# Five h matmuls instead of nine ahead of batch 1's first pair of score tiles

## The chip, the cores and the metric

The kernel runs on one core of a Trainium2 chip. The metric is the device time of one execution in microseconds. The engines have these names in the profile: PE is TensorE (matmuls), PEld its weight loads, ACT is ScalarE, DVE is VectorE, POOL is GpSimd and SP is SyncE. In this kernel POOL mainly issues loads, and SP issues transposing transfers and stores.

## What is computed

Sigmoid attention over 8 batches, 12 heads, 448 positions and 64 channels; its output, as 3584 rows of 768, goes through a two-matrix MLP with SiLU.

```
scores = q @ k.T / sqrt(64) - log(448)
attn   = 1 / (1 + exp(-scores))
x      = (attn @ v), heads side by side      # 3584 x 768
h      = x @ w_in                            # 768 -> 2048
out    = (h * sigmoid(h)) @ w_out            # 2048 -> 768
```

## The kernel before

A **group** g is four heads of one batch: three groups a batch (`NQ`), 24 in all. A group has seven **units** of scores (`NCH`), each a score tile: `scores` (L216) issues four matmuls of 64 rows into a double PSUM bank `psc` (L223) and then one sigmoid on ACT (L230), after which the bank is free. The units are numbered n = 7g + ch. Batch 0 has units 0 to 20 and batch 1 has 21 to 41.

When the seven units of a group are through, `values` (L238) multiplies them with v: 28 matmuls into two single banks `pav` (L254), which DVE copies, scaled, into xT (L265). Three such groups make one batch's xT.

The **h unit** (`h_unit`, L282) is one block of 128 of the 2048 columns of h for one batch: six matmuls (L286) into a single bank `ph`. For batch 0 ACT then takes the sigmoid (L300, into a buffer `tx`), and DVE multiplies it with the bank's content into gTr (L301); the bank is free after that. For batch 1 one SiLU on ACT (L305) does both. There are 16 h units a batch. The fifth and sixth matmul of a unit need the last group's xT of that batch.

PSUM has eight banks. In this phase two pairs are the double banks for score tiles, and four are single banks, shared by `ph`, `pav` and the transposes' outputs `ptrk` and `ptrq` (`pe_transpose`, L186: 14 matmuls, L194, and two copies on DVE, L201). A new tile in a single bank waits until the tile that had the bank before is read out. Which bank a tile takes follows from the order in which the tiles stand in the program.

The order is written out by hand. Units 0 to 23 come first, each followed by what the table `behind` (L699) says; behind units 21 and 23 the first four matmuls of h units 0 and 1 of batch 0 are issued (`begin`, the generators in `early`). Then h of batch 0 is woven between the remaining score tiles of batch 1:

- `first_h` (L551) is a generator that issues h matmuls, batch 0's units and then batch 1's, and yields 189 (ns) for each one.
- `stretch(stream, ns)` (L731) adds ns to `due` and takes matmuls from the generator until `done`, the sum of what they yielded, has reached `due`. What one stretch takes too much is taken off the next, since both sums run on.
- `burst(n)` (L741) issues the score tiles n and n + 1 and then, if a group is waiting for them, its values. Bursts are called here by their first unit: 24, 26, ... 40. Behind burst 26 and burst 30 stand the k and q transposes of group 5; in burst 28 the values of group 3, in burst 36 those of group 4.
- Ahead of burst 24 stands one stretch, and one more behind each of the nine bursts, so ten in all. Then come the values of group 5 (L761), the rest of batch 0's h, and all of batch 1's h.

```
754      stream = first_h()
755      stretch(stream, 1600)
756      for n in range(NT_B + 3, 2 * NT_B, 2):
757          burst(n)
758          if n in (26, 30):
759              transposes(5, "k" if n == 26 else "q")
760          stretch(stream, 1600)
761      values_if_any()
762      for _ in stream:
763          pass
```

While the generator runs, it also issues some DVE work for later phases: sums of parts of w_in (L324) behind batch 0's later h units, sums of w_out (L475) behind batch 1's. Loads of q, k, v and the weights are issued by POOL in the order of the program; each waits for an earlier load on the same semaphore and, where its buffer was in use, for the last reader.

Behind this phase stand three more rounds for the other six batches (output projection of finished batches woven with the attention of the next two), in the same order whatever the first phase does.

Of the kernel before, what the change touches and what calls it, by code (L numbers as in the profile page):

```python
# [17 lines left out]
def kernel(  # L18
# [532 lines left out]
    def first_h():  # L551
        for b in range(2):
            for fc in range(NFC):
                yield from early[fc] if b == 0 and fc < 2 else h_unit(b, fc)
                if b == 0 and fc >= 10 or b == 1 and fc < 6:
                    next(in_sums)
                if b == 0:
                    continue
                if fc >= 2:
                    next(sums)  # L560
                if fc in by_h1:
                    for name in ("k", "q"):
                        dma_transpose(by_h1[fc], name, nc.vector.tensor_copy)
                    if by_h1[fc] == 8:

                        nc.gpsimd.tensor_copy(gate, qkT["q", 8][:1, 0, :1])
                        for to in (9, 10, 11):
                            load("kq", to)

    def sets(m):  # L570
        for g in range(0, NCH - 1, 2):
            step = out_set(
                block(m, g), row_blocks(m, g), block(m, g + 1), row_blocks(m, g + 1)
            )
            for i, ns in enumerate(step):
                if m == 0 and g == 0 and i in (10, 14):
                    next(sums)
                if m == 0 and g == 0 and i in (20, 28, 36, 44):
                    next(in_sums)
                yield ns  # L580
        if m % 2 == 1:
            g = NCH - 1
            yield from out_set(
                kept, row_blocks(m - 1, g), block(m, g), row_blocks(m, g), m == B // 2 - 1
            )
# [145 lines left out]
    def stretch(stream, ns, spent=0):  # L731
        nonlocal done, due
        due += ns
        done += spent
        while done < due:
            step_ns = next(stream, None)
            if step_ns is None:
                return
            done += step_ns
# [12 lines left out]
        return with_values  # L752

    stream = first_h()
    stretch(stream, 1600)
    for n in range(NT_B + 3, 2 * NT_B, 2):
        burst(n)
        if n in (26, 30):
# [9 lines left out]
    for m in range(B // 2 - 1):  # L768
        banks_for_attention(3)
        nc.scalar.activation(warm, bias_s, AF.Sigmoid)  # L770
        stream = sets(m)
# [74 lines left out]
```

## Time and profile before

| | us |
|---|---|
| timed runs before, median of 3 | 369.14 |
| timed runs before, lowest and highest | 368.26, 369.56 |
| the profiled execution | 368.01 |
| its span, first to last instruction | 366.1 |
| granted TensorE clock over the span | 1.000 |
| from burst 24's first matmul to batch 1's sixth h matmul | 29.70 to 58.08 |

How to read the views: the page gives for each engine the time that it was busy and its share of the span. The chain of waits is followed back from the last instruction, at each step to what released it; each row has a start, a length and what ran. The timeline gives for each engine merged rows: start, length until the last one ends, line, operation, output and inputs, count, and in brackets the idle time just ahead with what ended it. TensorE's matmuls are pipelined: a matmul of 448 columns is shown 0.35 us long, while the next one starts 0.19 us after it. So the starts tell the pace, and an idle time in brackets is shorter than the time lost.

### The profile page before, as it was taken

What the parts mean: (1) busy time and instruction counts of PE and PEld (TensorE: products, weight loads), DVE (VectorE), ACT (ScalarE), POOL (GpSimd) and SP (SyncE); (2) the same over time, 40 slices, a digit from 0 to 9 for tenths busy, and PEclk for the clock granted to TensorE, in tenths of its full rate; (3) what the DMA queues carried; (4) which work ended last, traced back from release to release, by engine and by line L of the source; (5) the groups of instructions that cost most, each with busy time, mean ns of one, the idle gap of its engine ahead of it and who ended that gap; (6) DMA issues with size and microseconds to landing.
All of it is one profiled execution on the core that took longest, in us unless ns stands there. A gap on an engine that the chain in (4) does not pass through costs nothing.

```text
span 366.1 us, 7649 instructions
## 1 busy us (share of the span) xinstructions
PE 357.9 (98%) x3036; PEld 186.1 (51%) x3036; DVE 252.1 (69%) x459; ACT 249.9 (68%) x339; POOL 77.5 (21%) x116
## 2 busy tenths in 40 slices
PE   8899999999999999999999999999999999999995
PEld 5454445545544555555555545554555555555552
DVE  3665569777657587867675768795756677797763
ACT  6998885479998755687877856679998856640000
POOL 8556522040060172000023046000100000000000
PEclk9999999999999999999999999999999999999999
DMA  8999999989989599007879669902853120003333
GB/s 133 197 204 204 204 204 203 172 125 163 163 115 211 120 119 185 3 0 143 109 131 192 118 139 161 115 2 53 167 96 88 25 63 0 3 0 88 86 87 86
DMA packets 65859, 42.80 MB, mean 117 GB/s; under 512 B 36128, under 2 KB 62496, under 8 KB 65824
## 3 DMA queue, kind: packets, MB, share of 16 engines
q0 software_dynamic: 27072, 22.58, 42.4%
q1 hardware_dynamic: 38320, 19.34, 27.1%
q8 instruction: 24, 0.39, 0.4%
q10 hardware_dynamic: 432, 0.39, 0.3%
q14 instruction: 11, 0.09, 0.1%
HBM read 45.61 MB, written 11.01 MB: 155 GB/s over the span
## 4 chain that ended last, share of the span: by engine, by line
PE 83%; DMA 12%; POOL 3%; issue 1%; DVE 1%; POOLq 0%; DVEq 0%
PE po L502 37%; PE psc L223 9%; PE pa L376 8%; PE pd L376 8%; PE pc L376 7%; PE pav L254 7%; PE ph L286 5%; DMA w_out_sb<-in_moe_w_out_dram 5%; PE pb L376 4%; DMA w_in_sb<-in_moe_w_in_dram 3%; DMA vf<-in_v_dram 2%; DMA qf<-in_q_dram 2%; POOL kf L124 1%; POOL w_out_sb L162 1%; POOL vf L124 1%
## 5 line engine op out<-in xcount | busy, mean ns | idle before, releaser
L230 ACT ACTIVATE attnT<-psc,bias_s 128x896 f16<-128x896 f32 x168 | 158.1, 1008 | 22.2 <-PE psc L223 21.8
L502 PEld LDWEIGHTS <-S 128*128 128x128 f16 x448 | 41.6, 98 | 35.4 <-issue 7.3
L223 PE MATMUL psc<-qT,kT 64*64 64x448 f16 x672 | 50.5, 362 | 0.9 <-ACT attnT L230 0.6
L265 DVE TENSOR_SCALAR xT<-pav 128x448 f16<-128x448 f32 x48 | 27.7, 619 | 29.8 <-PE pav L254 29.8
L124 POOL DMA_DIRECT2D vf<-in_v_dram x24 | 17.3, 723 | 130.8 <-PE pav L254 118.5
L502 PEld LDWEIGHTS <-gTr 128*128 128x128 f16 x336 | 31.2, 98 | 26.6 <-issue 7.9
L502 PE MATMUL po<-T,S 128*128 128x384 f16 x224 | 41.7, 327 | 0.0
L376 PEld LDWEIGHTS <-w_in_sb 128*128 128x128 f16 x288 | 27.9, 98 | 26.7 <-issue 1.1
L502 PE MATMUL po<-w_out_sb,gTr 128*128 128x384 f16 x224 | 41.5, 327 | 0.0
L502 PE MATMUL po<-w_out_sb,S 128*128 128x384 f16 x224 | 40.6, 326 | 0.0
L286 PE MATMUL ph<-xT,w_in_sb 128*128 128x448 f16 x192 | 38.7, 353 | 0.1
L254 PE MATMUL pav<-attnT,vf 64*64 64x448 f16 x672 | 37.9, 350 | 0.4 <-DVE gTr L301 0.4
L376 PE MATMUL pa<-xT,w_in_sb 128*128 128x448 f16 x144 | 33.1, 353 | 0.0
L223 PEld LDWEIGHTS <-kT 64*64 64x64 f16 x672 | 17.7, 104 | 28.3 <-issue 22.5
L376 PEld LDWEIGHTS <-SI 128*128 128x128 f16 x216 | 21.1, 98 | 20.0 <-issue 0.5
L286 PEld LDWEIGHTS <-w_in_sb 128*128 128x128 f16 x192 | 17.9, 98 | 19.0 <-issue 3.7
L254 PEld LDWEIGHTS <-vf 64*64 64x64 f16 x672 | 20.8, 107 | 12.8 <-issue 3.2
L392 ACT ACTIVATE part<-pa 128x448 f32<-128x448 f32 x24 | 13.1, 544 | 18.8 <-PE pa L376 17.9
L502 PE MATMUL po<-T,gTr 128*128 128x384 f16 x112 | 22.1, 327 | 0.0
L370 ACT ACTIVATE gTr<-pc 128x448 f16<-128x448 f32 x24 | 13.1, 544 | 12.9 <-DVE pc L386 12.5
L386 DVE TENSOR_TENSOR part<-pb,part 128x448 f32<-128x448 f32 x24 | 14.9, 621 | 8.3 <-ACT part L392 5.0
L184 ACT ACTIVATE m<-po 128x384 f32<-128x384 f32 x1 | 0.5, 491 | 27.7 <-PE po L502 27.7
(76 smaller groups left out, 470.0 us busy)
## 6 DMA issues: line engine op xcount, KB each, us to landing
out_dram<-osb SPq DMA_DIRECT2D x52, 192.0 KB, 3.1
vf<-in_v_dram POOLq DMA_DIRECT2D x24, 224.0 KB, 7.0
kf<-in_k_dram POOLq DMA_DIRECT2D x23, 224.0 KB, 7.0
qf<-in_q_dram POOLq DMA_DIRECT2D x23, 224.0 KB, 7.5
w_in_sb<-in_moe_w_in_dram POOLq DMA_DIRECT2D x16, 192.0 KB, 8.2
w_out_sb<-in_moe_w_out_dram POOLq DMA_DIRECT2D x4, 768.0 KB, 14.9
out_dram<-osb SPq DMA_DIRECT2D x6, 96.0 KB, 2.1
kT<-kr SPq DMA_TRANSPOSE x18, 4.0
```

The source lines that it names most:

```text
L124: nc.gpsimd.dma_start(flat[name, g][:, :, c0:c1].rearrange("p i c d -> p i (c d)"), rows_in(name, g)[:, :, c0 * D : c1 * D],)
L162: nc.gpsimd.dma_start(w_out_sb[:, fcs, cols], moe_w_out[part * DFF // 2 : (part + 1) * DFF // 2, cols].rearrange("(fc p) e -> p fc e", p=P),)
L223: nc.tensor.matmul(psc[own, j, :S], qkT["k", g][rows, ch, own], qkT["q", g][rows, :, own], start=True, stop=True,)
L230: nc.scalar.activation(attnT[g, ch], psc[:, :, :S], AF.Sigmoid, bias=bias_s, scale=QKSCALE)
L254: nc.tensor.matmul(pav[half][j * D : (j + 1) * D, :S], flat["v", g][own, j, ch, :], at[own, j, :], start=(ch == 0), stop=(ch == NCH - 1),)
L265: nc.vector.tensor_scalar_mul(xT[b][:, half * NQ + iq, :], pav[half][:, :S], SX)
L286: nc.tensor.matmul(ph[:, :S], w_in_sb[:, cc, fc * P : (fc + 1) * P], xT[b][:, cc, :], start=(at == 0), stop=(at == NCC - 1),)
L370: nc.scalar.activation(gTr[:, r * NG + i, col + c * S : col + (c + 1) * S], h, AF.Silu, bias=0.0, scale=ISX)
L376: nc.tensor.matmul(to, w[:, n, i * P : (i + 1) * P], x[:, n], start=(start and n == 0), skip_group_check=not start, stop=(n == NQ - 1),)
L386: nc.vector.tensor_add(o, po, x)
L392: nc.scalar.activation(got[i, 1], bank[i, "a"], AF.Copy)
L502: nc.tensor.matmul(po[:, :NO2], a[:, fc, :], w[:, fc, :], start=(fc == 0), stop=(fc == NHC - 1))
```

## The change

The first of the ten stretches gets 900 ns instead of 1600.

```
--- before.py
+++ after.py
@@ -752,7 +752,7 @@
         return with_values
 
     stream = first_h()
-    stretch(stream, 1600)
+    stretch(stream, 900)
     for n in range(NT_B + 3, 2 * NT_B, 2):
         burst(n)
         if n in (26, 30):
```

At 189 a matmul the first stretch now ends after five matmuls (945) instead of nine (1701). As `due` and `done` run on, the later stretches change too: the ten had 9, 8, 9, 8, 9, 8, 9, 8, 9, 8 matmuls, and have 5, 9, 8, 9, 8, 9, 8, 9, 8, 8. Ahead of the values of group 5 stand 81 instead of 85, and behind them seven of batch 0's instead of three. The h matmuls keep their order among themselves, and so do the score tiles, values and transposes; the two sequences are shifted against each other by three or four matmuls. ACT's and DVE's work on the h units shifts with them, and so does the choice of single banks. The instructions on POOL and SP keep their order.

More of the change, by code (lines that the diff above doesn't have):

```diff
@@ L754 @@
     stream = first_h()
-    stretch(stream, 1600)
+    stretch(stream, 900)
     for n in range(NT_B + 3, 2 * NT_B, 2):
```

## The prediction

> **What bounds the kernel now.** I read the page first, then the chain of waits, then the timeline of each engine between 26 and 61 us.
>
> ```profile
> span 366.1 us, 7649 instructions
> ...
> PE 357.9 (98%) x3036; PEld 186.1 (51%) x3036; DVE 252.1 (69%) x459; ACT 249.9 (68%) x339; POOL 77.5 (21%) x116
> ```
>
> ```profile
> 25.02 8.27 DMA vf<-in_v_dram
> ...
> 38.80 17.14 DMA w_out_sb<-in_moe_w_out_dram
> 56.96 1.07 DVE xT L265 x2
> 58.08 17.38 PE ph L286 x91
> 75.45 2.27 PE po L502 x14
> ```
>
> From 58.08 on the chain is TensorE, with no transfer in these rows. 58.08 is the sixth h matmul of batch 1, released by the last scaled copy of the attention output. Whatever brings that matmul forward brings all behind it forward, if nothing there hangs on a clock time. So the question is how early TensorE reaches that point.
>
> ```profile
> 28.00:58.00 30.00, 29.19 (x277) 13.50 (x276) 16.75 (x32) 25.07 (x36) 13.38 (x19) 1.00 1.28 204
> ```
>
> In these 30 us (columns: PE, PEld, DVE, ACT and POOL busy, clock, DMA share, GB/s) TensorE counts as busy for 29.19. By that row alone 0.81 us could be won, and a gain of 0.81 would give 368.3 on the timed runs. The Trainium skill ("Perfetto Trace Analysis", section "Identifying the Most-Contended Engine") says that matmul busy time is a poor measure because matmuls are pipelined. The next view agrees with it here: the starts show more lost time than the busy share does. So I go by starts (first column of the timeline, TensorE alone).
>
> ```profile
> 29.70 0.57 PE L223 MATMUL psc<-qT,kT 64*64 64x448 f16 x8
> ...
> 31.83 0.71 PE L223 MATMUL psc<-qT,kT 64*64 64x448 f16 x8
> 32.47 0.41 PE L194 MATMUL ptrk<-ident,kf 128*64 128x128 f16 x8
> 33.25 0.36 PE L194 MATMUL ptrk<-ident,kf 128*64 128x128 f16 x6 [0.37 <-DVE gTr L301]
> 33.54 1.88 PE L286 MATMUL ph<-xT,w_in_sb 128*128 128x448 f16 x9
> 35.35 0.57 PE L223 MATMUL psc<-qT,kT 64*64 64x448 f16 x8
> 35.75 1.49 PE L254 MATMUL pav<-attnT,vf 64*64 64x448 f16 x28
> 37.18 1.69 PE L286 MATMUL ph<-xT,w_in_sb 128*128 128x448 f16 x8
> 38.79 0.57 PE L223 MATMUL psc<-qT,kT 64*64 64x448 f16 x8
> 39.30 0.58 PE L194 MATMUL ptrq<-ident,qf 128*64 128x128 f16 x14
> 39.81 1.88 PE L286 MATMUL ph<-xT,w_in_sb 128*128 128x448 f16 x9
> 41.62 0.57 PE L223 MATMUL psc<-qT,kT 64*64 64x448 f16 x8
> 42.12 1.69 PE L286 MATMUL ph<-xT,w_in_sb 128*128 128x448 f16 x8
> ...
> 46.13 0.57 PE L223 MATMUL psc<-qT,kT 64*64 64x448 f16 x8
> ...
> 47.34 1.51 PE L254 MATMUL pav<-attnT,vf 64*64 64x448 f16 x26 [0.45 <-DVE gTr L301]
> 48.78 1.69 PE L286 MATMUL ph<-xT,w_in_sb 128*128 128x448 f16 x8
> ...
> 54.83 1.56 PE L254 MATMUL pav<-attnT,vf 64*64 64x448 f16 x28
> 56.33 2.86 PE L286 MATMUL ph<-xT,w_in_sb 128*128 128x448 f16 x13
> ```
>
> Undisturbed lengths: eight h matmuls and the switch to scores 37.18 to 38.79, 1.61; nine 33.54 to 35.35, 1.81; so 0.19 to 0.20 each. A pair of score tiles 0.50 ahead of h (41.62 to 42.12), 0.51 ahead of transposes (38.79 to 39.30), 0.40 ahead of the value matmuls (35.35 to 35.75). Fourteen transposes 0.51 (39.30 to 39.81), 28 value matmuls 1.43 (35.75 to 37.18). Against these four places lose time. (a) The pair at 31.83 takes 0.64, so 0.13 too long. (b) The k transposes take 32.47 to 33.54, 1.07, so 0.56 too long. (c) Pair and values take 46.13 to 48.78, 2.65 where 35.35 to 37.18 took 1.83: 0.82 too long. (d) From 56.33 to 58.08 are eight h matmuls, 1.75 for 1.52: 0.23. Together 1.74.
>
> Places (b) and (c) wait for a single PSUM bank. An h unit that has just ended holds it until ScalarE's sigmoid (L300) and VectorE's product (L301) are through, and the sigmoid stands behind a pair of score tiles in ScalarE's order:
>
> ```profile
> 32.57 1.15 DVE L301 SCALAR_TENSOR_TENSOR gTr<-ph,tx 128x448 f16<-128x448 f32 x2 [2.27 <-ACT tx L300]
> ...
> 46.66 1.16 DVE L301 SCALAR_TENSOR_TENSOR gTr<-ph,tx 128x448 f16<-128x448 f32 x2 [1.61 <-ACT tx L300]
> ...
> 55.87 0.62 DVE L301 SCALAR_TENSOR_TENSOR gTr<-ph,tx 128x448 f16<-128x448 f32 x1 [0.58 <-ACT tx L300]
> 56.41 0.55 DVE L324 TENSOR_TENSOR SI<-w_in_sb 128x768 f16<-128x768 f16 x1
> ```
>
> **The change part by part.** It adds and removes no instruction of work; DMA queues keep their order. The ten stretches of h matmuls around the nine bursts go from 9,8,9,8,9,8,9,8,9,8 to 5,9,8,9,8,9,8,9,8,8; the four lost ones come behind the last values, seven instead of three. Four matmuls at 0.19 to 0.20 (0.76) are only moved, cost 0 in themselves, because TensorE runs both orders serially. What counts is which wait stands where, read from the built order.
>
> Place (b): the two k transposes take the banks of h units 0 and 1 instead of 1 and 2. Their sigmoids are the second row here, with the score tiles ahead of them in the first (ScalarE alone):
>
> ```profile
> 25.63 3.06 ACT L230 ACTIVATE attnT<-psc,bias_s 128x896 f16<-128x896 f32 x3
> 28.57 0.98 ACT L300 ACTIVATE tx<-ph 128x448 f16<-128x448 f32 x2
> 30.20 1.91 ACT L230 ACTIVATE attnT<-psc,bias_s 128x896 f16<-128x896 f32 x2 [0.65 <-PE psc L223]
> ...
> 38.90 0.55 ACT L300 ACTIVATE tx<-ph 128x448 f16<-128x448 f32 x1 [0.59 <-PE ph L286]
> ...
> 42.05 1.91 ACT L230 ACTIVATE attnT<-psc,bias_s 128x896 f16<-128x896 f32 x2 [0.35 <-PE psc L223]
> 43.85 0.54 ACT L300 ACTIVATE tx<-ph 128x448 f16<-128x448 f32 x1
> 44.27 1.92 ACT L230 ACTIVATE attnT<-psc,bias_s 128x896 f16<-128x896 f32 x2
> 46.05 1.00 ACT L300 ACTIVATE tx<-ph 128x448 f16<-128x448 f32 x2
> ```
>
> 28.57 plus 0.98 plus two products (1.15) is 30.7 at the latest, against transposes at 31.77 below. So 0.56 goes. Place (c): the values of group 4 take the banks of units 7 and 8 instead of 8 and 9; by the walk below unit 8 is through in time, so 0.82 goes. Place (d): batch 1's first unit comes after seven h matmuls instead of three, 0.8 us more cover, so 0.23 goes. Place (a) goes because the pair of 24 is earlier on ScalarE.
>
> New waits I look for by walking the new order. ScalarE's steps: a pair starts 0.43 after its first matmul (41.62 to 42.05), takes 1.91, and lets the next start 1.78 after it began (44.27 to 46.05); a sigmoid lets the next start after 0.42 (43.85 to 44.27) and can start 0.39 after its unit's last matmul (37.18 plus seven times 0.19 is 38.51; 38.90). Score tiles have two double banks: the second tile of a burst, 0.21 after the first, needs the pair before to be through.
>
> Burst 24: 29.70 less 0.76 is 28.94; both banks are free since 28.69 (25.63 plus 3.06). ScalarE is at two sigmoids until 29.42 (28.57 and twice 0.42), then at the pair to 31.33. H from 29.44, nine, burst 26 at 31.25; its second tile at 31.46 finds 31.33: no wait. Transposes 31.76, h 32.27 (eight), burst 28 at 33.89, values 34.29, h 35.72 (nine), burst 30 at 37.53, transposes, h 38.55 (eight), burst 32 at 40.16, h 40.67 (nine), burst 34 at 42.48, h 42.98 (eight), burst 36 at 44.59. ScalarE meanwhile: pairs from 31.68, 34.43, 37.96, 40.59, then sigmoids of units 7 and 8 from 42.37, pair of 34 from 43.21 to 45.12. So the second tile of 36, due 44.80, waits until about 45.17: 0.37 new. Unit 8's sigmoid starts at 42.79, its product is through near 44.1 (0.55 and 0.62), ahead of the values at 45.4. Then h 46.79 (nine), burst 38 at 48.60, h 49.1 (eight), burst 40 at 50.7, whose second tile waits 0.05 for pair 38 (49.03 plus 1.91), h 51.3 (eight), values 52.9, h 54.4 (1.50, as 54.83 to 56.33). The sixth h matmul of batch 1 is now the thirteenth: 54.4 plus twelve times 0.19 is 56.7. The trace has 58.08, so 1.3 to 1.4. As a sum: 1.74 less 0.37 less 0.05 is 1.32. I take 1.3.
>
> Costs that no row shows. The wait of tile 37 lies between 0 (ScalarE lets it through) and 0.82 (the longest such loss here); I take the walk's 0.37. ScalarE gets two more wait instructions; between 0 and 0.07 each (the pair at 30.20, which has such waits, began 0.50 after its matmul at 29.70, others 0.43), taken as 0. Transfers: v of group 3 lands at 33.29 (25.02 plus 8.27) and is now wanted at 34.29 instead of 35.75; 1.0 of cover is left of 2.5, priced 0. If it came later than that, each us is lost whole. From 58 on, the same order 1.3 earlier: 0, or down to a loss of the whole 1.3 if a landing there holds it.
>
> The profiled execution took 368.01, 1.9 around its span of 366.1, and lies 1.1 under the median of the three timed runs, 369.14. 368.01 less 1.3 is 366.7; on the runs, 369.14 less 1.3 is 367.8.
>
> **The rivals.** First, transfers pace the end of the stage. For it: the chain runs from the w_out transfer (landing 38.80 plus 17.14, 55.94) to the scaled copies and then 58.08, and the DMA share above is 1.28 throughout. Against it: the w_in sum at 56.41 starts 0.54 behind a product which itself waited for a sigmoid, and the built order has it wait for w_in, not w_out. If it holds, 58.08 stays: 369.1.
>
> Second, slower: ScalarE sets the pace of the bursts. TensorE meets the pair of 24 after five matmuls, so the 1.0 us that it arrived late (29.70, ScalarE's tiles done at 28.69) shrinks to 0.25, and without that cushion the second tile of each later burst waits. For it: ScalarE is busy 25.07 of 30, and a bare period needs 1.78 and one and a half sigmoids, 2.41, where TensorE needs 0.50 and 1.71, 2.21. Against: four of the nine bursts carry transposes or values, which let it catch up. It turns to a loss above a mean wait of 1.74 over nine, 0.19; at 0.37 in all nine it is 3.3 less 1.74, 1.6 slower: 370.7.
>
> Third, only the first bank wait goes. The values' wait at (c) returns because sigmoids run as late as before. Against: unit 8 ends a whole burst earlier than unit 9. Then the gain is 0.56 plus 0.13 less 0.05, 0.64: 368.5.
>
> **How the numbers follow.** Forecast 0.60; transfers pace 0.15; ScalarE paces 0.13; half gain 0.12. The timed runs spread from 368.26 to 369.56, so 0.3% (1.1 us) is about what can be told from no change; the gain of 1.3 is just past it. Faster: five sixths of the forecast and a little of the others, 0.55; slower: the second rival and a tail of the first, 0.14; same 0.31. The forecast's own range is 366.9 (all 1.74 gained, and half a us of spread) to 368.5; for 8 in 10 it runs from 366.5 to 369.8, past the first and third rival.
>
> **What would show it.** Right: no wait of transposes or values for L301 between 28 and 55, one score tile waiting about 0.4 near 45, and the long h run of batch 1 (58.08 now) near 56.8. Wrong: that row at 58 again; score tiles waiting for L230 in most bursts; values waiting for a product; or the start of L502's rows, 75.45 now, not moved with it.

## The result and the profile after

| | before | after |
|---|---|---|
| timed runs, median | 368.40 us (8 runs) | 366.81 us (8 runs) |
| ratio after to before, 95% interval | | 0.9959 [0.9948, 0.9971] |
| span of the execution that is read here | 366.1 us | 365.7 us |
| first h matmul behind score tile 23 to first output product | 27.03 to 75.29, 48.26 us | 27.92 to 74.83, 46.91 us |

The changed kernel is faster by 0.41%, or 1.5 us of 368.4, with an interval of 0.29% to 0.52%. The forecast was a gain of 1.3 us. One of the eight runs of the changed kernel, the profiled one, took 375.94 us at a granted clock of 0.949, so the ratio leaves it out and a second profile of the same kernel, at 0.998, is read instead.

The spans differ by 0.4 us only, because the same program does not start its h matmuls at the same time in each execution: 27.03 us into the span in the profile of before, 27.92 in this one. The last row of the table leaves that out. It is the measure used for every kernel below, called the **stage**: from the start of the h matmuls that follow score tile 23 to the start of the first L502 matmul, both read from TensorE's timeline. (The chain of waits in the prediction has L502 at 75.45: its rows begin only where the one before ends.) For the kernel before, the two rows of TensorE's timeline are these (start, length until the last one ends, line, output and inputs, count):

```profile
27.03 2.75 PE L286 MATMUL ph<-xT,w_in_sb 128*128 128x448 f16 x13
...
75.29 2.44 PE L502 MATMUL po<-w_out_sb,gTr 128*128 128x384 f16 x14
```

First the page of the changed kernel:

```profile
span 365.7 us, 7651 instructions
...
PE 357.8 (98%) x3036; PEld 186.1 (51%) x3036; DVE 252.4 (69%) x459; ACT 249.6 (68%) x339; POOL 77.5 (21%) x116
```

Every engine's busy time is within 0.3 us of before; no work was added or taken away. The two instructions more (7651 for 7649) are waits on ScalarE. Then TensorE's timeline, with the same places as in the prediction:

```profile
27.92 1.99 PE L286 MATMUL ph<-xT,w_in_sb 128*128 128x448 f16 x9
29.84 0.57 PE L223 MATMUL psc<-qT,kT 64*64 64x448 f16 x8
30.34 1.88 PE L286 MATMUL ph<-xT,w_in_sb 128*128 128x448 f16 x9
32.15 0.57 PE L223 MATMUL psc<-qT,kT 64*64 64x448 f16 x8
32.65 0.58 PE L194 MATMUL ptrk<-ident,kf 128*64 128x128 f16 x14
33.17 1.69 PE L286 MATMUL ph<-xT,w_in_sb 128*128 128x448 f16 x8
...
43.37 0.57 PE L223 MATMUL psc<-qT,kT 64*64 64x448 f16 x8
43.87 1.69 PE L286 MATMUL ph<-xT,w_in_sb 128*128 128x448 f16 x8
45.49 0.38 PE L223 MATMUL psc<-qT,kT 64*64 64x448 f16 x4
46.11 0.38 PE L223 MATMUL psc<-qT,kT 64*64 64x448 f16 x4 [0.24 <-ACT attnT L230]
46.30 1.52 PE L254 MATMUL pav<-attnT,vf 64*64 64x448 f16 x28
47.75 1.88 PE L286 MATMUL ph<-xT,w_in_sb 128*128 128x448 f16 x9
...
51.68 0.65 PE L223 MATMUL psc<-qT,kT 64*64 64x448 f16 x8
52.27 1.69 PE L286 MATMUL ph<-xT,w_in_sb 128*128 128x448 f16 x8
53.88 1.52 PE L254 MATMUL pav<-attnT,vf 64*64 64x448 f16 x28
55.34 4.90 PE L286 MATMUL ph<-xT,w_in_sb 128*128 128x448 f16 x25
```

The transposes and the values carry no bracket for L301 any more: their groups follow one another at the undisturbed lengths (32.65 to 33.17, 0.52; 46.30 to 47.75, 1.45). One score tile is issued in two rows, 45.49 and 46.11, with the wait for L230 between them. TensorE's waits by line between 26 and 80 us come to one row:

```profile
PE psc L223 <- ACT attnT L230: 0.2, 1, 0.2
```

And the chain of waits in the same stretch:

```profile
44.13 1.94 ACT attnT L230 x2
46.07 0.04 issue
46.11 0.38 PE psc L223 x4
...
55.40 19.59 PE ph L286 x103
74.99 2.27 PE po L502 x14
```

Where the chain of before ran over the w_out transfer and the scaled copies into 58.08, this one stays on TensorE from 46.11 on, without a break up to the first output product. Its 103 h matmuls take 19.59 us, 0.190 each, the undisturbed pace.

The busy time says less. In the same 30 us of the clock TensorE now counts 29.76 where it had 29.19:

```profile
28.00:58.00 30.00, 29.76 (x284) 13.73 (x285) 18.02 (x33) 26.21 (x37) 13.36 (x19) 1.00 1.28 204
```

### The profile page after: what moved, and what is told of

The parts are those of the page before. It is cut to its first block, busy times and chain, and to the rows that moved or that the text cites. A ratio compares the mean times of both kernels' runs of the same rounds, so it can differ in the third digit from the quotient of the medians.

```text
span 374.1 us, 7651 instructions
## 1 busy us (share of the span) xinstructions
PE 367.4 (98%) x3036; PEld 187.9 (50%) x3036; DVE 253.0 (68%) x459; ACT 249.6 (67%) x339; POOL 77.5 (21%) x116
## 4 chain that ended last, share of the span: by engine, by line
PE 93%; DMA 2%; POOL 2%; ACT 1%; issue 1%; DVE 0%; POOLq 0%; ACTq 0%
PE po L502 37%; PE psc L223 10%; PE ph L286 9%; PE pav L254 9%; PE pa L376 8%; PE pc L376 8%; PE pd L376 8%; PE pb L376 4%; DMA qf<-in_q_dram 2%; ACT attnT L230 1%; POOL kf L124 1%; POOL vf L124 1%; PE ptrq L194 0%; POOL qf L124 0%; PE ptrk L194 0%
## 5 line engine op out<-in xcount | busy, mean ns | idle before, releaser
L230 ACT ACTIVATE attnT<-psc,bias_s 128x896 f16<-128x896 f32 x168 | 158.0, 1007 | 23.2 <-PE psc L223 22.9
L502 PEld LDWEIGHTS <-S 128*128 128x128 f16 x448 | 42.2, 99 | 36.8 <-issue 7.6
L502 PEld LDWEIGHTS <-gTr 128*128 128x128 f16 x336 | 31.7, 99 | 27.9 <-issue 8.0
L502 PE MATMUL po<-T,S 128*128 128x384 f16 x224 | 42.8, 334 | 0.0
L502 PE MATMUL po<-w_out_sb,gTr 128*128 128x384 f16 x224 | 42.8, 334 | 0.0
L502 PE MATMUL po<-w_out_sb,S 128*128 128x384 f16 x224 | 41.9, 334 | 0.0
L286 PE MATMUL ph<-xT,w_in_sb 128*128 128x448 f16 x192 | 39.9, 362 | 0.0
L254 PE MATMUL pav<-attnT,vf 64*64 64x448 f16 x672 | 39.0, 359 | 0.0
L376 PE MATMUL pa<-xT,w_in_sb 128*128 128x448 f16 x144 | 34.3, 362 | 0.0
L502 PE MATMUL po<-T,gTr 128*128 128x384 f16 x112 | 22.7, 334 | 0.0
L386 DVE TENSOR_TENSOR part<-pc,part 128x448 f32<-128x448 f32 x24 | 15.0, 624 | 7.1 <-PE pc L376 6.5
```

The lines of the kernel that those rows point to most:

```text
L230: nc.scalar.activation(attnT[g, ch], psc[:, :, :S], AF.Sigmoid, bias=bias_s, scale=QKSCALE)
L254: nc.tensor.matmul(pav[half][j * D : (j + 1) * D, :S], flat["v", g][own, j, ch, :], at[own, j, :], start=(ch == 0), stop=(ch == NCH - 1),)
L286: nc.tensor.matmul(ph[:, :S], w_in_sb[:, cc, fc * P : (fc + 1) * P], xT[b][:, cc, :], start=(at == 0), stop=(at == NCC - 1),)
L376: nc.tensor.matmul(to, w[:, n, i * P : (i + 1) * P], x[:, n], start=(start and n == 0), skip_group_check=not start, stop=(n == NQ - 1),)
L386: nc.vector.tensor_add(o, po, x)
L502: nc.tensor.matmul(po[:, :NO2], a[:, fc, :], w[:, fc, :], start=(fc == 0), stop=(fc == NHC - 1))
```

## The experiments

The theory, called theory A in the expectations: the gain is made of four separate places, each a wait of TensorE. One is for ScalarE at a score tile, two are for a PSUM bank, one is for the scaled copies into xT; the two bank waits go or come according to which unit's bank is taken. The rivals are those of the prediction: that the transfers (theory B) or ScalarE set the pace, or that only the first bank wait goes. Theory C is that the gain comes from ScalarE's earlier start on the first pair; with none ahead of burst 24 it stands for the rival in which ScalarE sets the pace. Most of the edits shift h matmuls between stretches; "n" is the burst, and 900 in place of 1600 takes about four matmuls out of one stretch.

| run | ratio of time, 95% | stage, us | against 48.26 |
|---|---|---|---|
| the changed kernel again | 0.9962 [0.9950, 0.9974] | 27.92 to 74.83, 46.91 | -1.35 |
| front half alone | 0.9988 [0.9979, 0.9997] | 27.48 to 75.04, 47.56 | -0.70 |
| shift behind burst 28 | 1.0013 [1.0004, 1.0021] | 27.79 to 76.18, 48.39 | +0.13 |
| the same, one bank skipped | 0.9970 [0.9958, 0.9982] | 27.84 to 75.45, 47.61 | -0.65 |
| shift behind burst 38 | 1.0012 [1.0004, 1.0021] | 27.09 to 75.72, 48.63 | +0.37 |
| seven ahead of burst 24 | 1.0012 [1.0003, 1.0021] | 26.96 to 75.71, 48.75 | +0.49 |
| none ahead of burst 24 | 1.0037 [1.0024, 1.0049] | 27.43 to 77.06, 49.63 | +1.37 |
| five, and ten ahead of burst 36 | 0.9953 [0.9939, 0.9966] | 27.67 to 74.19, 46.52 | -1.74 |
| changed kernel, beside the next | 0.9967 [0.9955, 0.9979] | 28.23 to 75.13, 46.90 | -1.36 |
| five and ten, beside it | 0.9952 [0.9939, 0.9964] | 27.46 to 73.99, 46.53 | -1.73 |
| the kernel before again | one run, 368.23 us | 27.17 to 75.43, 48.26 | 0.00 |

In all these traces the part behind the stage has the same length: the span less the first output product's start is 290.77 to 290.87 us. So whatever the order of the h matmuls does, it has done by then.

**The changed kernel again.** No edit; it gave the lines above.

> The changed kernel once more, for an undisturbed profile. Theory A (waits for single PSUM banks go): batch 1's sixth h matmul at 56.6 to 56.9 (58.08 before); no transposes and no value matmuls waiting for L301; one score tile (37) waiting 0.3 to 0.4 for L230 near 45; time 1.3 to 1.6 us under before. Theory B (transfers pace the stage): the matmul stays at about 58. Theory C (ScalarE, started earlier, is what gains): score tiles wait in most bursts.

Measured -1.35 in the stage and 0.9962 in time (1.4 us). The sixth h matmul of batch 1 starts at 57.62 and not at 56.6 to 56.9, because this whole stage starts 0.89 later; less that it is 56.73. The theory's sum stands. The kernel before was run once more too:

> The kernel before itself, for a second profile of it: from the first h matmul behind unit 23 to the first output product 48.26 again within 0.05, with the same two waits for L301, while the time at which that first h matmul comes may differ by up to 0.9, as it does between the profiles so far.

Its stage was 48.26 again, to the hundredth, with a start at 27.17 instead of 27.03. A difference of 0.1 us in the stage can therefore be told, while the intervals of the time reach 0.3 to 0.5 us to either side.

**The front half alone.** Five matmuls ahead of burst 24, and the four put back behind burst 28, so that everything from burst 30 on has the old order.

```
-    stretch(stream, 1600)
+    stretch(stream, 900)
...
-        stretch(stream, 1600)
+        stretch(stream, 2300 if n == 28 else 1600)
```

> Five matmuls in the first stretch, and the four given back in the stretch behind burst 28, so that from burst 30 on the order is the one before. Theory A: the long wait of the k transposes goes (0.56) and the score tile's at 31.8 (0.13), while the values of group 4 still take unit 9's bank and wait as before (0.82) and the last wait for xT stays (0.23): sixth h matmul at about 57.4, 0.7 us under before. Theory C (the early start of ScalarE is what gains): the whole 1.3 to 1.6, at 56.7.

Measured -0.70. Its transposes run undisturbed (32.22 to 32.73), and the wait of the values of group 4 is there as before. This row of its waits is the only one up to the first output product:

```profile
PE pav L254 <- DVE gTr L301: 0.4, 1, 0.4
```

The first two places are worth 0.69 by the prediction's lengths (0.13 and 0.56), whatever the rest does. Theory C had the whole gain here, 1.3 to 1.6, and half of it came.

**The shift behind burst 28.** The other half: nine ahead of burst 24 as before, and the four taken out behind burst 28.

```
-        stretch(stream, 1600)
+        stretch(stream, 900 if n == 28 else 1600)
```

> Nine matmuls in the first stretch as before, the four taken from the stretch behind burst 28 instead, so that from burst 30 on the order is that of the changed kernel. Theory A: the k transposes wait as before (0.56, with 0.13 ahead of it), the values of group 4 take units 7 and 8's banks and do not wait, tile 37 waits about 0.4, the wait for xT goes: sixth h matmul at about 57.4, 0.6 to 0.7 us under before. Theory C: no gain, since the first pair comes as late as before.

At batch 1's sixth h matmul the expectation held: it starts at 58.17, 30.38 behind the start of the stage, where before needs 31.05 (27.03 to 58.08). That is 0.67 won, though the first pair came as late as before, so theory C fails here too. And yet the whole stage is 0.13 longer. TensorE's waits by line, then its timeline at the end of the stage, then ScalarE's timeline with its step for the last h unit show why:

```profile
PE po L502 <- ACT gTr L305: 0.6, 1, 0.6
PE ptrk L194 <- DVE gTr L301: 0.4, 1, 0.4
PE psc L223 <- ACT attnT L230: 0.2, 1, 0.2
```

```profile
76.18 2.11 PE L502 MATMUL po<-w_out_sb,gTr 128*128 128x384 f16 x12 [0.63 <-ACT gTr L305]
```

```profile
75.58 0.54 ACT L305 ACTIVATE gTr<-ph 128x448 f16<-128x448 f32 x1 [0.59 <-PE ph L286]
```

The first output product starts 0.06 behind the end of that step (75.58 plus 0.54 is 76.12). It takes the first of the two single banks of the next phase, and here this is the bank of the last h unit of all, h31 in the built order. Before and in the changed kernel it is that of h28. From the sixth h matmul to the first product are 18.01 us here and 17.21 before (58.08 to 75.29): 0.80 lost, 38 us behind the shortened stretch (from 37.93). Over all the traces this length is 17.21, except in the three orders whose built program gives the first product h31's bank, this one and the ones with seven and with none ahead of burst 24: there it is 18.01.

**The same, one bank skipped.** To show that it is the bank, the same kernel with one more single bank taken from the rotation ahead of the output products, by a write of one column that nobody reads.

```
         banks_for_attention(3)
+        if m == 0:
+            nc.vector.memset(one_bank("skip")[:, :1], 0.0)
```

> The variant with the four matmuls taken behind burst 28 gained 0.66 up to batch 1's sixth h matmul, as forecast, but lost 0.8 at the first output product, whose bank was that of batch 1's last h unit. Here a one-column VectorE fill takes that bank first, so that the product gets the other single bank. Theory A (it is the bank): the 0.63 wait ahead of the first product goes, its start comes 17.2 behind the sixth h matmul instead of 18.0, time 0.6 to 0.7 us under before. If something else held that product (weights, VectorE's sums): 18.0 again, and the time as for that variant.

The wait went, and the half gain came through whole: the stage is 0.65 shorter than before, and the time 0.9970 where the same order of matmuls without the skip had 1.0013. In the built order the fill takes h31's bank and the product that of h29. The ratio says 1.1 us (0.7 to 1.5), a little more than the stage, the medians 0.8; the stage is the finer measure.

```profile
75.45 1.79 PE L502 MATMUL po<-w_out_sb,gTr 128*128 128x384 f16 x10
```

The two halves, -0.70 and -0.65, add up to the -1.35 of the changed kernel.

**The shift behind burst 38.** Here the four come out only behind burst 38, after the two bank waits, which stay.

```
-        stretch(stream, 1600)
+        stretch(stream, 900 if n == 38 else 1600)
```

> Nine matmuls first, the four taken from the stretch behind burst 38. Theory A: both bank waits stay, the wait for xT (0.23) goes, but score tile 41 now comes 0.76 earlier and waits about 0.6 for ScalarE to be through with tile 39: sixth h matmul at 58.3 to 58.5, same or up to 0.4 us over before. If it is only the four matmuls more behind the last values that help: 0.2 under before. Theory C: no gain.

Measured +0.37. The second tile of burst 40 meets ScalarE at work:

```profile
50.95 1.12 PE L286 MATMUL ph<-xT,w_in_sb 128*128 128x448 f16 x5
52.00 0.38 PE L223 MATMUL psc<-qT,kT 64*64 64x448 f16 x4
52.84 0.38 PE L223 MATMUL psc<-qT,kT 64*64 64x448 f16 x4 [0.45 <-ACT attnT L230]
53.15 1.69 PE L286 MATMUL ph<-xT,w_in_sb 128*128 128x448 f16 x8
```

From 52.00 to 53.15 are 1.15 us for a pair that needs 0.50, so 0.65 lost against 0.23 won at the scaled copies and 0.05 at the last values (1.45 for 1.50), which makes the 0.37. A stretch of five between two bare bursts is too short for ScalarE; the changed kernel puts its five ahead of the first burst, where ScalarE had been waiting.

**Seven ahead of burst 24.** The middle way, meant to give the banks a different phase and no tile wait.

```
-    stretch(stream, 1600)
+    stretch(stream, 1300)
```

> Seven matmuls in the first stretch (1300). The k transposes get the banks of units 0 and 1 and the values of group 4 those of units 7 and 8, as with five, but the first output product gets the last h unit's bank. Theory A: no wait for L301, so about 1.3 gained up to the sixth h matmul, 0.8 lost ahead of the first product: 0.4 to 0.6 us under before. If fewer matmuls ahead of the first pair are what gains, in proportion: half of the changed kernel's gain, 0.7, up to the sixth h matmul.

This was a miss: +0.49 instead of a gain, and up to the sixth h matmul 0.31 won instead of about 1.3. The 0.80 at the first output product came as expected, but there was a second bank wait that the expectation had not priced:

```profile
53.34 0.38 PE L254 MATMUL pav<-attnT,vf 64*64 64x448 f16 x2
54.54 1.51 PE L254 MATMUL pav<-attnT,vf 64*64 64x448 f16 x26 [0.83 <-DVE gTr L301]
55.98 1.31 PE L286 MATMUL ph<-xT,w_in_sb 128*128 128x448 f16 x6
```

The values of group 5 take 2.64 instead of 1.50. They use the banks of units 12 and 13 in both orders. But before, unit 13 ends ahead of burst 40; here its last matmul is the first one behind that burst, so its sigmoid stands behind the burst's pair. ScalarE alone, before and then here, the pair of burst 40 in L230:

```profile
52.63 0.98 ACT L300 ACTIVATE tx<-ph 128x448 f16<-128x448 f32 x2
53.48 1.93 ACT L230 ACTIVATE attnT<-psc,bias_s 128x896 f16<-128x896 f32 x2
```

```profile
51.48 1.92 ACT L230 ACTIVATE attnT<-psc,bias_s 128x896 f16<-128x896 f32 x2
53.26 1.00 ACT L300 ACTIVATE tx<-ph 128x448 f16<-128x448 f32 x2
```

Together with 0.23 at an h unit behind the transposes (32.06 to 32.80, 0.74 for 0.51) the losses are 0.80 plus 1.14 plus 0.23, 2.17, against the 1.74 won: 0.43, near the measured 0.49.

**None ahead of burst 24.** The change taken to its end: the first burst comes at once.

```
-    stretch(stream, 1600)
+    stretch(stream, 0)
```

> No h matmuls in the first stretch, so the pair of 24 comes at 27.9 while ScalarE is still at tile 23. Theory A: tile 25 waits 0.6 for ScalarE, the values of group 3 wait 0.3 for unit 2, small waits besides, together 1.2 where before lost 1.74 plus 0.1: sixth h matmul 0.6 to 0.8 earlier than before, counted from the start of h unit 1; the first product gets the last unit's bank and loses 0.8, so the time is that of before within 0.3 us. Theory C (ScalarE paces once the cushion is gone): score tiles wait in most bursts, 1 us or more over before.

A miss in the total, +1.37. The sixth h matmul of batch 1 comes 0.57 later than before, counted from the start of the stage, where 0.6 to 0.8 earlier was expected: the expectation did not have the wait of group 5's values. The waits show the same two bank places as with seven, and one score tile:

```profile
PE pav L254 <- DVE gTr L301: 0.8, 1, 0.8
PE po L502 <- ACT gTr L305: 0.6, 1, 0.6
PE psc L223 <- ACT attnT L230: 0.5, 1, 0.5
```

The tile lost 0.66 (28.29 to 29.45, 1.16 for 0.50), the values of group 3 0.46 (34.37 to 36.25, 1.88 for 1.42), the values of group 5 1.15 and the first product 0.80: 3.07 less 1.74 is 1.33. The only tile that waits with a row of its own is the first; with no cushion at all ScalarE still does not hold up most bursts. This speaks against the rival in which ScalarE paces the bursts, even in this order.

**Five, and ten ahead of burst 36.** The changed kernel loses 0.41 at tile 37. Two more h matmuls ahead of that burst, and two fewer behind it, should take that wait away.

```
-    stretch(stream, 1600)
+    stretch(stream, 900)
...
-        stretch(stream, 1600)
+        stretch(stream, 2000 if n == 34 else 1200 if n == 36 else 1600)
```

> Five matmuls in the first stretch and two more in the one ahead of burst 36 (ten), two less in the next. Theory A: the one wait left, of score tile 37 for ScalarE (0.3 to 0.4), goes too and no other comes: 1.7 us under before. If ScalarE sets the pace: the wait moves to another burst and the time stays that of the changed kernel, 1.4 under before.

It did: stage -1.74, and no row of waits at all for TensorE between 26 and 80 us. The burst and its values now take 43.62 plus the ten matmuls to 45.62, 0.43 for the pair, 1.45 for the values:

```profile
43.62 2.06 PE L286 MATMUL ph<-xT,w_in_sb 128*128 128x448 f16 x10
45.62 0.62 PE L223 MATMUL psc<-qT,kT 64*64 64x448 f16 x8
46.05 1.52 PE L254 MATMUL pav<-attnT,vf 64*64 64x448 f16 x28
47.50 1.50 PE L286 MATMUL ph<-xT,w_in_sb 128*128 128x448 f16 x7
```

It was then run beside the changed kernel, both against the same runs of before.

> The changed kernel again, beside the evened one on the same chip: 1.3 to 1.5 us under before.

> Five first, ten ahead of burst 36, seven behind it, again: theory A says 0.37 less than the changed kernel beside it, the wait of tile 37 that it does not have.

The stages repeated within 0.01 (46.90 and 46.53). TensorE's busy time in the window of the prediction is now the window:

```profile
28.00:58.00 30.00, 30.00 (x287) 13.98 (x285) 18.39 (x34) 26.48 (x38) 13.12 (x18) 1.00 1.28 204
```

The medians were 366.96 and 366.66, ratios 0.9967 [0.9955, 0.9979] and 0.9952 [0.9939, 0.9964]. This is the fastest version that was run, by 0.37 us in the stage; in the time the two intervals overlap, so only the traces tell them apart.

## Why the prediction was right

**The sum, place by place.** (a) The pair ahead of the transposes takes 0.50 (32.15 to 32.65) instead of 0.64, so 0.14 went, as against 0.13. (b) The transposes take 0.52 instead of 1.07: 0.55 for 0.56. (c) Pair and values take 2.26 (45.49 to 47.75) instead of 2.65. Of this the values' wait is gone whole (1.45), and the pair lost 0.41 (0.81 for 0.40), where the walk had 0.37. (d) The long row of h from 55.34 has no break, so 0.23 went. The wait of tile 41 is 0.09 (51.68 to 52.27, 0.59 for 0.50) where the walk had 0.05. Two small losses of before were not on the list: the pair at 43.74 took 0.59 and takes 0.50 now, and the last values took 1.50 and take 1.46 now. Together 0.14 plus 0.55 plus 0.82 plus 0.23 plus 0.13, less 0.41 and 0.09, is 1.37; measured 1.35, forecast 1.32. The sum of the prediction missed 0.13 of gains and 0.08 of losses, so 0.05 was left between 1.32 and 1.37: part of the agreement is that two errors had opposite signs.

**The walk over ScalarE.** It put pair 34 at 43.21 and the end of that pair at 45.12, in a trace whose stage began at 27.03. With the 0.89 by which this trace begins later, that is 44.10 and 46.01; measured are 44.13 and 46.07. The steps taken from the trace of before (0.43, 1.78, 0.42 and 0.39) were good enough to carry over six bursts.

**The sixth h matmul of batch 1.** Forecast 56.7; it starts at 57.62, that is 56.73 by the clock of the earlier trace. The absolute number was read off one trace, and should have been given from the start of the stage.

**The rivals.** Transfers do not pace the end of the stage: with the same queues the sixth h matmul came 29.70 behind the start instead of 31.05, and the chain no longer touches a transfer there. ScalarE does not pace the bursts: of nine, one waits 0.41 and one 0.09. The values' wait at (c) did not come back, so the gain is not the half one.

**The time.** Forecast 367.8, measured 366.81. Of the 1.0 between them 0.74 lies in the base: the first three runs of before had a median of 369.14, all eight 368.40. The rest is the gain itself, 1.3 against 1.6 by these medians, 1.5 by the ratio and 1.35 by the trace, which is inside the ratio's interval of 1.1 to 1.9. For the same reason 366.81 lies just under the forecast's own range of 366.9 to 368.5, inside the wider one from 366.5.

**What was priced at nothing.** The earlier need for v of group 3 cost nothing, as priced: those values start 0.41 behind the first matmul of their pair (34.78 to 35.19), against 0.40 undisturbed. "From 58 on, the same order 1.3 earlier: 0" was right too, but by luck: it named a landing as what could hold it. The shift behind burst 28 shows that the bank under the first output product could have, for 0.80, and then the change would have gained 0.55 only. The prediction does not speak of that bank. That the changed kernel keeps it at h28 is how the rotation falls for this count, not something that the edit provides for.

## What to carry to other kernels

Where banks go round in program order, an edit that shifts one sequence of work against another changes which unit each later consumer waits for, up to the next stage and not only around the edit. So list for every taker of a bank whose bank it gets and when that one is evicted, in both orders, before pricing the edit; most of the losses here were 0.5 to 1.2 us each, where all the matmuls that were moved take 0.76. And measure a stage from its own first instruction, since the start can differ by more than the effect.

## What the runs showed of the hardware that was not expected

The same instructions up to there do not bring the first h matmul of the stage at the same time: it starts between 26.96 and 28.23 us into the span over these twelve traces, a spread of 1.27 us, as large as the gain studied. In the changed kernel's two traces, at 27.92 and 28.23, the chain of waits before the stage runs over one long transfer of k:

```profile
8.30 9.84 DMA kf<-in_k_dram
```

```profile
8.30 10.14 DMA kf<-in_k_dram
```

The same k transfer, 9.38 to 9.76 us long, stands in the chain of three more: the front half, the skipped bank, and the first run of five and ten. In all five the stage starts 9.78 to 9.80 behind its landing. It is not the whole cause, though: the shift behind burst 28 starts at 27.79 with no transfer of such a length in its chain. In the repeat of before, at 27.17, a transfer of q of 9.25 us stands in that place, and in the earliest of all (seven ahead, 26.96) there is none. What makes it long in some executions was not tried and stays open. From the stage's start on, against that, repeats of a kernel agree within 0.01 us over 47 us.
